# Attention and feed-forward on one core: half of batch 0's first layer in block form, other column pieces of the first weights, squares on either engine, and a new order of all operations

## The chip, the cores and the metric

The kernel runs on one core of a Trainium2 chip. The metric is the device time of one execution in microseconds (us); the median of three runs is compared. The engines are called by the names of the profile: PE (TensorE, matrix products), ACT (ScalarE), DVE (VectorE), POOL (GpSimd, which here issues the loads and waits at a few gates) and SP (SyncE, which issues stores and the transposes by DMA).

## The reference

For 8 batches of 12 heads with 448 positions of 64 numbers, attention with a squared relu in place of the softmax, then a feed-forward network with a gelu:

```python
def _attn_ref(q, k, v):
    S = q.shape[2]
    scale = 1.0 / np.sqrt(q.shape[-1])
    scores = scale * np.matmul(q, k.transpose(0, 1, 3, 2))
    attn = np.maximum(scores, 0.0) ** 2 / S
    return np.matmul(attn, v)

def reference(q, k, v, moe_w_in, moe_w_out):
    a = _attn_ref(q, k, v)                       # (8, 12, 448, 64)
    x = a.transpose(0, 2, 1, 3).reshape(8 * 448, 768)
    h = x @ moe_w_in                             # 768 x 2048
    g = 0.5 * h * (1.0 + erf(h / np.sqrt(2)))
    return g @ moe_w_out                         # 2048 x 768
```

Inputs and output are float32. The kernel multiplies in bfloat16 and sums in float32.

## The kernel before, in words

**Attention.** The heads of a batch form three groups of four, and the 448 keys seven blocks of 64. Q and K are first turned so that the 64 numbers of a head lie on partitions: for batches 0 and 1 by PE (`tp`, lines 619 and 647), with an eviction by ACT or DVE to `qT` and `kT`; from batch 2 on by DMA. A step (`add_steps`) is one group and one block of keys: PE makes the scores in PSUM (`ps`, line 751) with 64-row, 64-column tiles of its array, four products side by side; a relu with the scale takes them to a bfloat16 tile `a_sq` (128 partitions by 896), on ACT (line 768) or DVE (line 770); a square in place follows on DVE (line 777). Batch 0 works in halves of 224 positions. When the seven steps of a group are squared, `add_av` makes the attention product (`pav`, line 824, 28 matmuls), and two copies take it to `xT`, the input of the first layer.

**The first layer** takes 768 numbers to 2048, in 16 column blocks of 128 (called m). It is made in one of two ways.

* Plain (`add_f1`): for one block and all positions, or for two blocks and one half of the positions, six matmuls per block sum over the 768 rows in PSUM (`psh`, line 884), and a gelu on ACT (line 894) writes `h_sb`.
* Block form (`add_early` for batches 1 to 6, `add_blocks` for batch 7): weights and input are each cut in two by two quarters, and seven products of quarters take the place of eight. For this DVE makes sums of weight quarters (`ws`, line 955, by `add_wsums`; one kind is written over a quarter of `win_sb` itself), and sums of input quarters (`t1_x` to `t4_x`, line 998). A unit (`add_unit`) covers two blocks of the upper half of the columns, say 0 and 1, and the two that lie eight further. Its products (`pe`, line 1039, matmuls of 224 columns) share three PSUM banks, and between products ACT or DVE passes a partial sum to `part` (copies, lines 518 and 520; adds on DVE, line 1077); ACT makes four gelus (line 1089). Units come in pairs y = 0, 1; two pairs (h = 0 and h = 1) make a batch. The sums of weights hold one h at a time for the second and fourth kind, so they are made again as h changes.

In the kernel before, batch 0 is plain throughout: blocks 0 to 5 in halves of the positions, blocks 6 to 15 whole.

**The second layer** takes 256 positions at a time (`add_group`, products `pso` at line 1366), in a block form as well.

**Loads.** The first weights come in five pieces of columns (`WINS`, `add_win`), each with three DMAs on POOL's queue; the sums of weights wait for all five.

**The order.** Every operation is created with what it depends on and the engines that may do it. The table `ORDER` then lists all of them: a letter for the engine (P or Q for PE, A for ACT, D for DVE, G for POOL, S for SP; Z is a filler for PE) and the operation's number. Each engine works strictly in this order, and an instruction that waits holds up all behind it. So ACT or DVE is chosen for each relu, copy and eviction by the table alone.

Of the kernel before, what the change touches and what calls it, by code (L numbers as in the profile page):

```python
# [10 lines left out]
AF = mybir.ActivationFunctionType  # L11
# [11 lines left out]
DM = H * D  # L23
# [11 lines left out]
EARLY = (1, 2, 3, 4, 5, 6)  # L35
NB = 512
WINS = (2, 2, 4, 4, 4)
# [15 lines left out]
HALF_M = 6  # L53
# [30 lines left out]
A10 D13 G0 G1594 Z1024 P14 P11 D15 G1 G3 G4 G7 D12 A16 P17 P36 D18 A37 P21 G118 G2 P19 P42 P39 P33  # L84
D22 G117 P23 D20 A43 D40 P48 A34 A49 D24 P25 P54 A55 D26 Z672 P63 P66 D38 A67 D41 D50 P51 A52 P29
D35 P27 D28 D30 D44 P57 D53 D68 P31 D32 A64 A58 P131 P81 G121 A82 P45 A46 A47 P69 A70 D132 D59 G6
P129 P84 A85 P90 A91 G125 G126 D65 G5 D130 P156 D71 D157 P78 A79 Q72 D73 P93 A94 P102 D83 G8 G122
G120 G124 G119 G128 P111 D112 P137 D113 P108 A74 D95 G123 G9 G127 D138 G236 P174 D56 A103 A109 P139
D86 P75 A175 A76 D110 D140 P133 P60 P105 D77 P96 A61 A62 P168 A106 G235 D80 P135 D136 D104 A97 P171
G238 A172 P87 D134 P141 G147 G148 G150 D92 A169 A88 A89 A142 P159 A160 D98 P162 P99 D107 D163 G151  # L90
Q114 A100 A101 P198 A199 D115 D116 P183 A184 P165 A166 D176 P145 A146 S228 S229 G153 P240 A241 D173
D158 G154 D200 P213 A214 P180 D170 A181 P222 P252 A253 D167 S230 P250 A251 D223 P195 D161 A196 P207
D164 D208 P177 P186 A187 D182 D209 D178 D179 P210 D197 P262 A263 D215 A211 G234 P256 P192 D193 P189
P216 P254 A190 A257 S231 P219 A255 D191 D349 D350 D212 P204 A220 P244 S232 S233 D194 A217 P248 A245
A249 D218 D185 P260 A205 P242 A243 D188 P201 A202 D224 G237 G149 G152 A261 G155 D221 D206 P225 D387
D226 D203 A227 D345 D346 D348 P246 A247 D351 P264 G239 G266 P353 P370 A354 P360 P143 A144 G267 P377
P356 D425 D426 A371 D427 A361 A378 D347 P258 A259 D352 P373 D388 P382 P355 A374 P379 D383 D380 P372
P365 A357 P362 D358 P385 A386 D375 A359 D366 D363 P391 P408 A364 G268 P368 A369 P398 P415 P393 P410
D431 A265 D428 A399 D389 P403 D390 A409 A392 P394 D413 P411 A416 P420 D396 D432 A384 A367 P282 Q273
A412 D395 G269 P400 P417 D421 A274 D404 A405 P437 A283 A422 A438 P276 A277 D433 S453 D418 D401 S454  # L100
D434 P291 D429 D435 A292 P406 P423 A424 D430 A407 A402 P439 G270 P288 A289 P285 A286 D293 P297 D298
D440 P441 A442 P315 A316 P279 D284 A414 D287 D436 P300 D290 P443 D444 D275 A280 D281 P445 P447 D278
P309 A301 D446 D448 S451 A397 G271 P303 A419 A381 P294 A376 D469 D470 S455 A310 D295 A304 S456 S457
S458 D305 P312 D311 P449 D450 S452 A313 D302 D314 A296 P321 D471 A322 D323 P324 A325 P306 A307 D308
D317 P473 A474 P339 G459 P327 A328 P475 P477 P336 D299 G462 D472 A340 D329 D476 A337 D338 A478 P330
P318 A331 G272 P333 D334 A319 A320 D332 P479 P498 A499 P492 G465 D341 P489 A490 P481 A493 P495 A496
D335 D326 P342 A343 P507 P504 A505 D480 D482 P485 D344 D561 D562 D564 D563 A508 P565 G460 G461 D509
P582 A583 P572 P589 D494 P585 D586 P567 P584 D500 A566 P568 D573 P591 D570 A590 D592 P594 D587 P577
D599 A569 P483 D578 G463 P601 A588 P618 D486 D595 A602 P574 P597 A598 G464 D600 D491 G466 G467 D575
P603 A576 P620 D484 D619 S488 P580 A581 S635 D606 D497 Q501 A593 S636 A502 S637 D623 P604 P621 D506  # L110
D503 A622 P608 P625 A624 A605 D651 D652 P513 A514 D515 Q510 P522 P610 S638 A596 P627 D626 D628 G641
G644 A609 P613 D611 D653 P630 A511 A512 A523 A571 D614 Q516 A517 P519 D520 P616 P633 D631 A632 D654
D524 A617 P655 A634 P657 P528 D656 D529 P531 A532 D533 S487 G468 P549 A550 D658 P659 D521 A607 D518
P543 A544 P540 A660 D541 P537 A538 P661 P663 D662 A579 D539 P694 P555 D530 D551 A629 P525 A612 A526
D664 A695 D545 D527 P665 D666 A556 D542 P667 A615 D671 P709 A710 D672 P534 P546 S669 P706 A547 D535
A536 A707 P675 D668 P677 P552 S639 S640 G647 P703 D696 P691 D673 G642 D676 D674 D678 P679 A680 D553
A692 P681 D548 D557 P697 D554 P558 G643 G645 G646 D708 A704 P715 D698 P700 D682 D559 P683 A701 D560
P767 P784 D684 D763 A716 D785 A768 D705 D764 P687 P769 P786 P774 D711 D766 P787 A788 D765 A775 D772
P685 A773 G648 D693 D688 D789 G649 S690 P770 A771 D699 P791 D686 P779 A790 Q727 D728 P724 S837 S838
A792 D702 A725 P793 P776 D794 A795 P796 P803 P820 D777 S839 P799 S840 A778 G843 P782 D801 D797 A800  # L120
A783 D804 S670 Q712 P718 G846 D821 D780 A798 A719 A713 A714 P805 P822 P806 D802 P823 D825 A824 Q748
P721 D808 P810 D729 P827 A807 P812 D726 A749 A828 D722 P757 Q730 P829 A811 D717 D853 D854 D830 S689
D813 A731 S841 P832 D833 P857 D858 A826 P818 D732 P815 A809 P835 D720 D816 D855 A831 A819 P859 D860
A758 D759 P861 A817 D862 A836 A834 P896 A897 P733 P739 D740 P863 D856 A734 P742 P905 A906 P745 P865
D898 D864 D866 G650 P867 D735 D750 A781 P869 D868 D723 D870 S872 A814 D873 D874 S842 A746 D747 P920
A921 P736 A737 D738 P751 D876 A743 D744 A752 D753 P877 P879 P911 P754 A878 D880 D875 D741 P908 A755
D756 P881 A882 D909 A912 D922 P883 P893 D894 D884 P899 A900 D910 D895 P760 P926 A761 A762 P923 A924
P885 D886 G849 P887 P902 D913 D901 G844 D888 D965 A927 D967 A903 P917 D907 P889 D890 P969 P986 G845
G847 G848 A918 S1039 D904 Q935 D936 P929 A970 A930 P914 A915 A916 Q941 P971 P988 D966 D968 D919 P976
P993 D925 A987 D991 G850 A994 D937 P972 P989 A990 D977 G851 P981 S892 S1040 D974 A942 P998 A973  # L130
D1003 P1005 P1022 D999 A1000 A1023 P978 D982 D979 A1006 P1007 P1024 D1027 P1008 A992 S1041 A980 Q932
D1010 P995 A1028 P1025 A1026 A933 D996 A997 D1009 P1012 P1029 A1030 D1004 D934 P1014 P1031 D1032
A975 D1013 P1001 A1002 D1015 P1059 D1060 P984 A1016 A985 D931 A1033 S871 G1045 P1020 P1037 A1038
P1034 D1057 P1017 A1021 P950 P1098 P1063 D1055 D1056 D1018 S891 A983 D1035 D951 S1042 S1043 G1048
A1019 P1061 P959 A1099 D1100 P956 D928 D1062 A957 D960 A1036 P938 A939 A940 P1101 D1102 P944 A945
D1058 D946 P1065 A1064 P947 P953 P1119 A1011 D1066 D961 P1067 D958 G852 A948 D1068 A1120 P1069 D943
P1095 A954 D955 D1070 A1096 D1097 D949 D1075 D952 P1122 P1125 A1126 S1073 A1123 P1071 D1072 D1076
P1079 D1080 P1128 D1078 S1074 P1107 A1108 P962 D963 A964 P1110 P1081 D1082 P1083 A1129 A1084 P1104
D1077 D1111 S1044 G1051 G1046 P1113 A1114 P1085 P1173 D1112 A1105 D1106 D1169 P1087 D1109 P1190
P1171 P1188 A1172 A1189 D1086 D1088 P1091 D1103 D1167 D1168 P1178 D1170 D1176 D1092 P1195 A1196  # L140
P1089 P1174 P1191 D1193 A1194 D1130 D1090 Q1134 A1177 A1135 D1115 P1116 D1124 D1179 D1127 A1192
Q1143 D1117 P1183 D1118 A1144 P1200 P1137 A1138 D1175 Q1131 D1201 D1184 A1185 G1047 G1049 P1197
P1180 A1132 A1202 G1050 D1205 D1181 A1182 D1198 D1206 S1241 P1207 P1224 D1208 P1209 P1226 A1225
Q1155 A1156 A1199 P1186 D1212 P1210 D1229 D1145 P1203 A1230 A1204 D1133 P1227 D1228 A1211 P1214
P1231 A1187 P1216 P1233 Q1146 D1139 A1213 D1121 A1232 A1147 D1136 P1140 A1141 Q1149 A1142 D1215
P1219 P1236 D1217 A1218 D1234 A1235 D1150 D1237 A1238 P1222 P1239 G1052 D1220 S1242 Q1152 A1223
D1153 A1240 G1053 A1221 P1270 A1271 P1279 A1280 S1093 S1094 P1276 P1251 A1252 P1158 P1161 D1247
S1243 D1248 A1277 P1253 D1249 D1162 D1157 A1159 P1255 D1254 D1160 P1257 S1244 D1148 D1256 P1259
P1267 P1273 A1274 D1163 D1154 D1151 D1258 D1260 A1268 D1250 P1164 A1165 D1278 P1285 D1281 A1166
D1339 D1340 P1263 A1286 S1245 P1345 P1343 P1360 A1361 P1350 D1272 P1367 P1362 D1287 D1342 D1344  # L150
A1351 P1346 A1368 P1363 A1364 P1372 A1347 D1365 P1261 A1366 D1341 D1275 D1348 P1352 P1369 D1370
D1353 P1355 D1356 S1246 G1595 P1379 P1396 G1054 P1358 D1373 A1371 A1357 D1262 P1375 A1374 A1380
# [252 lines left out]
def kernel(  # L405
# [185 lines left out]
    def add_win(i):  # L591
# [3 lines left out]
        for x in range(m, m + WINS[i]):  # L595
            ld_win[x] = o
# [1108 lines left out]
```

## Time and profile before

| | |
|---|---|
| median of 3 runs | 365.86 us (365.82 to 366.21) |
| the profiled execution | 365.36 us |
| its span, first to last instruction | 363.5 us |
| mean granted TensorE clock | 0.999 |
| instructions | 9137 |
| PE / DVE / ACT busy | 352.7 / 312.9 / 233.4 us |

The profile is one execution. "Busy" counts the time in which at least one instruction of an engine is under way; matmuls overlap in the pipeline, so the mean duration of one is longer than busy time by count. The chain of waits follows the work that ended last backwards. A group is named by the line of the program, the engine and the tiles, output first.

### The profile page before, as it was taken

Reading aid. Unit: us, or ns where it says so; the run is one execution under the profiler, and the core shown is the slowest. Engines: PE = TensorE matmul, PEld = TensorE weight load, DVE = VectorE, ACT = ScalarE, POOL = GpSimd, SP = SyncE. Lnnn points to the kernel's source line nnn. Section 1 sums busy time; section 2 is a strip of 40 time slices with the busy share of each in tenths; the row PEclk is TensorE's granted clock in tenths of the full one; section 3 lists DMA queues with packets and bytes.
Section 4 is the critical chain, followed back from the end, with each engine's and each line's share of the span. In section 5 each row is a group of like instructions: output and inputs, shape, how many; then the busy total and the mean of one; then the engine's idle time right before and its main releaser. Section 6 shows DMA issues by size and latency. Waiting matters only on the chain.

```text
span 363.5 us, 9137 instructions
## 1 busy us (share of the span) xinstructions
PE 352.7 (97%) x3805; PEld 244.2 (67%) x3805; DVE 312.9 (86%) x544; ACT 233.4 (64%) x396; POOL 102.9 (28%) x138
## 2 busy tenths in 40 slices
PE   8889999999999999999999999999999999999995
PEld 4557569855588655886557975678669855798663
DVE  3999988999789899899999799899896999687753
ACT  4998844899846795567675869457854885344200
POOL 8565715284192105610074100470100000000000
PEclk9999999999999999999999999999999999999999
DMA  9999999999999808997199941699900201021213
GB/s 176 200 200 204 202 204 155 172 143 168 155 161 173 157 21 107 142 208 107 56 81 167 183 74 45 94 129 181 136 2 0 88 2 44 3 88 43 88 43 132
DMA packets 124361, 43.01 MB, mean 118 GB/s; under 512 B 102688, under 2 KB 120992, under 8 KB 124320
## 3 DMA queue, kind: packets, MB, share of 16 engines
q0 software_dynamic: 85328, 22.47, 66.4%
q1 hardware_dynamic: 38448, 19.50, 26.3%
q8 instruction: 30, 0.49, 0.6%
q10 hardware_dynamic: 544, 0.46, 0.4%
q14 instruction: 11, 0.09, 0.1%
HBM read 45.61 MB, written 11.01 MB: 156 GB/s over the span
## 4 chain that ended last, share of the span: by engine, by line
PE 83%; DVE 8%; ACT 4%; DMA 2%; issue 1%; POOL 1%; DVEq 0%; POOLq 0%; ACTq 0%
PE pso L1366 36%; PE pe L1039 21%; PE ps L751 8%; PE pav L824 8%; PE psh L884 5%; PE pb L1190 4%; DVE a_sq L777 2%; DMA nq<-in_q_dram 2%; DVE part L1077 2%; DVE part L518 2%; ACT part L520 2%; ACT h_sb L1089 1%; ACT a_sq L768 1%; DVE qT L518 1%; DVE ws L955 0%
## 5 line engine op out<-in xcount | busy, mean ns | idle before, releaser
L768 ACT ACTIVATE a_sq<-ps 128x896 bf16<-128x896 f32 (+1 forms) x151 | 121.9, 861 | 26.1 <-PE ps L751 25.3
L777 DVE TENSOR_TENSOR a_sq<-a_sq 128x896 bf16<-128x896 bf16 x169 | 98.2, 615 | 1.9 <-ACT a_sq L768 1.5
L1366 PEld LDWEIGHTS <-s_sb 128*128 128x128 bf16 x456 | 42.5, 98 | 31.9 <-issue 6.0
L1039 PEld LDWEIGHTS <-win_sb 128*128 128x128 bf16 x576 | 54.4, 98 | 7.9 <-issue 6.3
L751 PE MATMUL ps<-qT,kT 64*64 64x448 bf16 (+1 forms) x756 | 50.0, 338 | 2.4 <-DVE kT L518 0.8
L1077 DVE TENSOR_TENSOR part<-pe,part 128x448 f32<-128x448 f32 x72 | 42.4, 618 | 7.6 <-PE pe L1039 5.9
L1366 PEld LDWEIGHTS <-h_sb 128*128 128x128 bf16 x336 | 31.8, 98 | 22.6 <-issue 4.1
L520 ACT COPY part<-pe 128x448 f32<-128x448 f32 x54 | 27.5, 535 | 29.7 <-PE pe L1039 20.6
L1089 ACT ACTIVATE h_sb<-part 128x448 bf16<-128x448 f32 x72 | 39.9, 580 | 8.8 <-DVE part L1077 8.7
L1039 PEld LDWEIGHTS <-ws 128*128 128x128 bf16 x432 | 41.2, 98 | 2.9 <-issue 2.0
L1366 PE MATMUL pso<-wout_sb,s_sb 128*128 128x384 bf16 (+2 forms) x232 | 41.1, 321 | 0.0
L1366 PE MATMUL pso<-wout_sb,h_sb 128*128 128x384 bf16 x224 | 41.1, 327 | 0.0
L1366 PE MATMUL pso<-t_sb,s_sb 128*128 128x384 bf16 x224 | 41.1, 326 | 0.0
L558 POOL DMA_DIRECT2D nk<-in_k_dram x36 | 34.7, 968 | 10.4 <-DMA wout_sb<-in_moe_w_out_dram 7.9
L770 DVE TENSOR_SCALAR a_sq<-ps 128x896 bf16<-128x896 f32 (+1 forms) x35 | 33.5, 967 | 4.7 <-PE ps L751 4.1
L824 PE MATMUL pav<-a_sq,v_sb 64*64 64x448 bf16 (+1 forms) x756 | 36.4, 329 | 0.5 <-ACT a_sq L768 0.4
L751 PEld LDWEIGHTS <-kT 64*64 64x64 bf16 x756 | 19.0, 105 | 23.8 <-issue 17.9
L1039 PE MATMUL pe<-t_x,win_sb 128*128 128x224 bf16 x288 | 32.6, 259 | 1.3 <-DVE part L518 0.6
L1039 PE MATMUL pe<-t_x,ws 128*128 128x224 bf16 x288 | 31.2, 259 | 0.4 <-ACT part L520 0.4
L708 POOL COPY gate<-qT 128x16 bf16<-128x16 bf16 x10 | 3.0, 299 | 101.1 <-DMA qT<-nq 101.1
L1039 PE MATMUL pe<-xT,win_sb 128*128 128x224 bf16 x288 | 31.5, 259 | 0.0
L1400 DVE TENSOR_TENSOR osb<-pso,p_sb 128x384 f32<-128x384 f32 x42 | 23.2, 552 | 8.8 <-PE pso L1366 7.8
(71 smaller groups left out, 411.8 us busy)
## 6 DMA issues: line engine op xcount, KB each, us to landing
out_dram<-osb SPq DMA_DIRECT2D x19, 384.0 KB, 2.6
nq<-in_q_dram POOLq DMA_DIRECT2D x38, 112.0 KB, 5.9
nk<-in_k_dram POOLq DMA_DIRECT2D x36, 112.0 KB, 5.6
v_sb<-in_v_dram POOLq DMA_DIRECT2D x5, 672.0 KB, 7.5
v_sb<-in_v_dram POOLq DMA_DIRECT2D x9, 224.0 KB, 7.9
win_sb<-in_moe_w_in_dram POOLq DMA_DIRECT2D x8, 192.0 KB, 8.7
wout_sb<-in_moe_w_out_dram POOLq DMA_DIRECT2D x4, 384.0 KB, 12.6
wout_sb<-in_moe_w_out_dram POOLq DMA_DIRECT2D x1, 1536.0 KB, 15.6
```

What stands on the lines that cost most here:

```text
L520: A.copy(dst, src)
L558: nc.gpsimd.dma_start(nk[b][:, g0, :, e], rows[:, e].rearrange("p (i d) -> p i d", d=D))
L751: nc.tensor.matmul(side(ps, e)[64 * j : 64 * j + 64, x * w : x * w + w], kT[r, g, i * 128 + 64 * j : i * 128 + 64 * j + 64], moving, start ...
L768: A.activation(to, x, AF.Relu, scale=c_att)
L770: V.tensor_scalar(to, x, c_att, 0.0, op0=mybir.AluOpType.mult, op1=mybir.AluOpType.max,)
L777: V.tensor_mul(box["a2"][:, :, :used], ar, ar)
L824: nc.tensor.matmul(side(pav[0], e)[o2 : o2 + 64, :w], vt[b][r, 2 * g + e, bass.ts(i, D)], box["a2"][r, e, o : o + w], start=(i == 0), stop ...
L1039: nc.tensor.matmul(bank[name][:, y, z * HS : z * HS + HS], w[:, k, bass.ts(mm, 128)], right()[:, k], start=first and k == 0 and z == 0, st ...
L1077: V.tensor_add(get(to), ps(name), get(other))
L1089: A.activation(h_ring()[:, m : m + 2, o + half[c].start : o + half[c].stop], src().rearrange("p (x n) -> p x n", x=2), AF.Gelu,)
L1366: nc.tensor.matmul(box[bank][:, n0:n1], left()[:, kf], right()[:, kf, n0:n1], start=bool(need) and kf == 0, stop=kf == K2 - 1, skip_group_ ...
L1400: V.tensor_add(out()[:, n0:n1], box[bank][:, n0:n1], other()[:, n0:n1])
```

## The change

Four things change together.

1. Batch 0 joins the batches of the block form with the half h = 1: blocks 4 to 7 and 12 to 15, two units. The other eight blocks stay plain: 0, 1 and 8 to 11 in halves of the positions, 2 and 3 whole. The sum of weights that overwrites a quarter of `win_sb` waits for these plain products where it must. The sums for h = 1 are made for batch 0 and used by batch 1 first; in the kernel before they were made for batch 1.
2. The pieces of the first weights hold other columns: blocks 0 and 1, 6 and 7, 8 to 11, 2 to 5, 12 to 15. Their sizes stay.
3. The square may be done by ACT, as an activation, or by DVE.
4. The table of the order is new from its first line to its last, with 1618 operations for 1596.

```diff
-EARLY = (1, 2, 3, 4, 5, 6)
+EARLY = (0, 1, 2, 3, 4, 5, 6)
-WINS = (2, 2, 4, 4, 4)
+WINS = ((0, 2), (6, 8), (8, 12), (2, 6), (12, 16))
-HALF_M = 6
+HALF_M = (0, 8, 10)
 ORDER = """
-A10 D13 G0 G1594 Z1024 P14 P11 D15 G1 G3 G4 G7 D12 A16 P17 P36 D18 A37 P21 G118 G2 P19 P42 P39 P33
...
+G0 G1616 G1 G3 G4 G7 D13 Z1024 A10 G118 A16 G2 P14 D15 P11 D12 P17 D18 P19 D20 P42 A43 P36 A37 P33
...
     def add_win(i):
-        m = sum(WINS[:i])
-        c = slice(128 * m, 128 * (m + WINS[i]))
-        o = dma(lambda: load_win(c), DM * 128 * WINS[i] * 4, issues=3)
-        for x in range(m, m + WINS[i]):
+        m0, m1 = WINS[i]
+        c = slice(128 * m0, 128 * m1)
+        o = dma(lambda: load_win(c), DM * 128 * (m1 - m0) * 4, issues=3)
+        for x in range(m0, m1):
             ld_win[x] = o
...
             def fn_mul(e_, box=box, used=used):
                 ar = box["a2"][:, :, :used]
-                V.tensor_mul(box["a2"][:, :, :used], ar, ar)
+                if e_ == "ACT":
+                    A.activation(ar, ar, AF.Square)
+                else:
+                    V.tensor_mul(ar, ar, ar)
...
-            o3 = sch.add((("DVE", d, d + 0.12),), fn_mul, [o2], bias=bias)
+            d2 = 0.07 + 2 * used / 1200
+            o3 = sch.add(
+                (("DVE", d, d + 0.12), ("ACT", d2, d2 + 0.12)), fn_mul, [o2], bias=bias
+            )
...
+    PLAIN = [(m + x, h) for m in HALF_M for x in range(2) for h in range(2)]
+    PLAIN += [(m, None) for m in (2, 3)]
...
     def add_early(b):
-        done = [o for (bb, *_), o in F1.items() if bb < EARLY[0]]
+        done = [F1[0, m, h] for m, h in PLAIN] if b else []
...
-        for h in ((0, 1), (1, 0))[at % 2]:
+        for h in ((1,), (1, 0), (0, 1))[0 if b == 0 else 2 - at % 2]:
...
-    for m in range(0, HALF_M, 2):
+    for m in HALF_M:
         add_f1(0, m, 0, bias=F1_BIAS)
...
-    for m in range(0, HALF_M, 2):
+    for m in HALF_M:
         add_f1(0, m, 1, bias=F1B_BIAS)
-    for m in range(HALF_M, KF):
+    for m in (2, 3):
         add_f1(0, m, bias=F1B_BIAS)
+    flow = [o for o in add_early(0)]
```

Line numbers of the changed kernel are higher than those of the profile by 1 (from line 518 on), 4 (the square on DVE stands at 781, on ACT at 779), 7 (from 824), 9 (from 998) and 10 at the end.

Counted over the whole program: 61 of the 169 squares now stand on ACT; 57 relus stand on DVE where 35 did (halves and split ones counted as they are issued) and 125 on ACT where 151 did. PE has 48 `psh` matmuls of 448 columns fewer and 84 `pe` matmuls of 224 more. POOL's list of loads is the same in kind and size, row by row.

Two places show how the order differs. The first is DVE around the last squares of batch 1's attention (`a_sq`), where the sums of first weights (`ws`, `win_sb`) and of inputs (`t_x`) come in. Before:

```order
L770 TENSOR_SCALAR a_sq<-ps 128x896
L777 TENSOR_TENSOR a_sq<-a_sq 128x896
L955 TENSOR_TENSOR ws<-win_sb 128x3x512
L955 TENSOR_TENSOR ws<-ws,win_sb 128x1536
L777 TENSOR_TENSOR a_sq<-a_sq 128x896 x8
L955 TENSOR_TENSOR ws<-win_sb 128x3x512
L518 CAST xT<-pav 128x448 x2
L998 TENSOR_TENSOR t_x<-xT 128x672
L998 TENSOR_TENSOR t_x<-xT,t_x 128x672 x2
L955 TENSOR_TENSOR ws<-win_sb,ws 128x1536
```

In the changed kernel, at the same place:

```order
L771 TENSOR_SCALAR a_sq<-ps 128x896
L781 TENSOR_TENSOR a_sq<-a_sq 128x896 x3
L962 TENSOR_TENSOR ws<-win_sb 128x3x512
L781 TENSOR_TENSOR a_sq<-a_sq 128x896 x3
L962 TENSOR_TENSOR ws<-ws,win_sb 128x1536
L1007 TENSOR_TENSOR t_x<-xT 128x672
L519 COPY part<-pe 128x448
L962 TENSOR_TENSOR ws<-win_sb 128x3x512
L1086 TENSOR_TENSOR part<-pe,part 128x448
L781 TENSOR_TENSOR a_sq<-a_sq 128x896
L962 TENSOR_TENSOR win_sb<-win_sb 128x3x512
L962 TENSOR_TENSOR ws<-win_sb,ws 128x1536
```

The last squares of batch 1 now stand between the sums for batch 0's block products, and a copy and an add of those products stand ahead of the very last one.

The second place is ACT at the end of batch 1's attention, with its relus (`a_sq` from `ps`), gelus (`h_sb`), casts of the attention product (`xT`) and copies of block products (`part`). Before:

```order
L768 ACTIVATE a_sq<-ps 128x896 x2
L894 ACTIVATE h_sb<-psh 128x2x224
L894 ACTIVATE h_sb<-psh 128x448
L768 ACTIVATE a_sq<-ps 128x896
L894 ACTIVATE h_sb<-psh 128x2x224
L520 CAST xT<-pav 128x448
L894 ACTIVATE h_sb<-psh 128x448
L520 CAST xT<-pav 128x448
L894 ACTIVATE h_sb<-psh 128x448
L520 COPY part<-pe 128x448
```

In the changed kernel:

```order
L769 ACTIVATE a_sq<-ps 128x896
L521 COPY part<-pe 128x448
L769 ACTIVATE a_sq<-ps 128x896
L521 CAST xT<-pav 128x448 x2
L769 ACTIVATE a_sq<-ps 128x896
L779 ACTIVATE a_sq<-a_sq 128x896 x2
L521 COPY part<-pe 128x448 x4
L521 CAST xT<-pav 128x448 x2
L1098 ACTIVATE h_sb<-part 128x2x224 x3
```

The last relus are followed by two squares on ACT, for which the last attention product of batch 1 waits, and copies of block products of batch 0 stand before and behind them.

More of the change, by code (lines that the diff above doesn't have):

```diff
@@ L89 @@
[L89 to L113, printed above, removed]
@@ new lines @@
+D1110 P1111 D1100 P1113 G1074 D1128 A1211 D1215 P1165 A1194 G1075 D1198 D1112 S1115 A1199 A1166
+A1167 D1114 P1138 D1190 D1192 S1264 S1265 Q1153 S1096 P1200 P1217 P1196 P1213 A1139 A1154 D1140
+A1218 Q1177 A1201 D1227 A1197 P1159 A1160 P1205 A1214 P1222 D1191 A1216 P1229 P1246 P1219 D1223
+A1224 S1116 D1206 D1178 A1247 D1220 P1231 S1266 P1248 D1251 S1267 A1230 G1617 P1232 P1249 A1161
+A1221 P1202 A1233 D1234 A1235 P1225 A1250 D1228 A1207 D1158 D1203 A1226 P1236 P1253 A1152 P1238
+D1146 D1237 D1239 P1208 P1241 P1244 A1209 A1204 D1155 P1255 A1240 D1242 A1243 A1252 P1171 S1268
@@ new lines @@
+D1254 D1256 Q1168 A1169 P1258 D1172 P1261 A1257 Q1174 A1245 A1262 D1259 A1260 P1162 P1295 A1173
+A1163 G1076 P1183 A1184 D1175 P1273 D1269 A1274 D1270 P1275 A1164 P1301 D1271 A1179 D1176 P1180
+A1302 A1303 D1276 P1277 P1279 D1296 D1185 D1278 P1281 P1289 A1181 A1182 D1272 D1170 D1280 D1282
+A1290 P1307 D1308 P1186 A1187 D1188 D1361 P1292 A1293 D1294 P1298 P1285 A1297 P1365 P1382 D1286
+D1362 D1364 A1299 D1300 P1367 A1383 P1372 P1389 A1366 D1370 A1291 D1373 A1390 D1363 P1283 A1371
+D1284 P1384 D1387 P1385 P1368 A1369 P1304 Q1313 A1305 D1399 D1386 P1377 P1394 D1306 D1395 A1396
@@ new lines @@
+A1388 P1401 P1418 A1419 P1391 D1378 P1403 P1420 A1402 P1374 D1309 P1404 P1421 D1400 D1406 D1423
+A1424 P1408 P1425 D1375 D1392 A1376 D1475 A1405 A1422 A1393 D1409 P1397 A1398 D1426 A1379 P1410
+D1314 P1427 D1428 P1380 A1381 S1288 P1430 A1429 D1411 A1412 P1413 D1414 P1340 D1431 A1341 Q1310
+A1311 D1435 D1315 P1355 A1356 P1328 A1329 P1416 P1433 A1417 P1439 P1352 S1287 P1343 D1312 A1434
+D1436 D1438 A1432 P1322 D1437 D1353 A1415 P1441 D1323 A1440 P1443 P1325 D1344 P1316 D1442 A1444
+P1346 A1347 P1445 P1331 D1326 A1407 D1327 D1324 P1337 D1446 A1342 D1457 A1332 A1333 P1447 A1348
@@ new lines @@
+P1555 A1554 P1557 A1494 D1518 P1521 A1514 D1556 P1543 D1541 A1542 P1546 A1491 D1522 D1524 A1525
+D1547 A1548 S1474 A1558 P1559 P1526 P1529 D1530 S1453 D1560 A1531 P1536 A1537 D1544 A1545 P1561
+D1562 D1527 A1528 P1563 D1564 P1519 A1520 D1569 P1565 S1567 D1570 P1573 A1574 D1566 S1568 D1571
+P1575 D1572 P1577 D1576 D1578 P1579 P1581 D1580 P1583 D1582 P1585 D1591 D1584 S1587 D1589 D1590
+D1586 S1588 P1593 P1595 A1594 D1596 P1597 A1598 S1609 P1599 D1592 P1601 D1600 P1603 D1602 P1606
+S1610 D1604 S1611 P1605 D1607 S1612 D1608 S1613
@@ L1595 @@
     add_v(3, 0, G)
-    flow, plans = [], {}
+    plans = {}
     F1B = {2: 1, 3: 2, 4: 3, 5: 4, 6: 5, 7: 6}
```

124 lines of the change are left out of this document (63 added, 61 removed).

## The prediction, made before the changed kernel was run

> **What bounds the kernel now.** I read the page's first part, then a table by stages, then the chain of waits, the groups of instructions and the waits. The first part gives the span and the engines' shares.
>
> ```profile
> span 363.5 us, 9137 instructions
> PE 352.7 (97%) x3805; PEld 244.2 (67%) x3805; DVE 312.9 (86%) x544; ACT 233.4 (64%) x396; POOL 102.9 (28%) x138
> ```
>
> By its average TensorE (PE) is the bound. The table by stages says where that is not the whole story; its columns are the stretch, its length, and each engine's busy time with its instructions.
>
> ```profile
> 4.90:26.00 21.10, 17.48 (x461) 12.08 (x463) 19.16 (x38) 19.28 (x29) 14.59 (x21) 1.00 1.39 196
> 26.00:49.10 23.10, 23.02 (x310) 14.63 (x305) 21.67 (x37) 18.62 (x30) 13.48 (x17) 1.00 1.29 204
> 49.10:80.00 30.90, 30.21 (x304) 23.31 (x297) 27.91 (x42) 21.14 (x40) 15.07 (x20) 1.00 1.68 166
> 80.00:130.00 50.00, 49.45 (x513) 33.12 (x512) 44.98 (x80) 37.83 (x63) 19.44 (x25) 1.00 1.51 153
> 130.00:330.00 200.00, 198.74 (x2024) 140.31 (x2022) 179.66 (x315) 128.57 (x223) 36.55 (x47) 1.00 0.72 91
> ```
>
> From 4.9 to 26 us PE lacks 3.6 us, while VectorE (DVE) and ScalarE (ACT) are each 91% busy: this stretch is theirs. From 26 us on PE is busy almost throughout, but DVE stays at 90 to 94% up to 130 us. Only after that has it room. The chain of waits names the milestones (start, length, what).
>
> ```profile
> 47.85 2.77 PE pav L824 x56
> ...
> 55.88 1.15 PE pe L1039 x12
> 57.02 1.14 PE psh L884 x6
> ...
> 74.96 1.30 PE pso L1366 x8
> 76.26 0.69 PE ps L751 x12
> 76.96 1.41 PE pso L1366 x8
> ...
> 340.20 19.65 PE pso L1366 x128
> ```
>
> The 56 matmuls at 47.85 are the last two attention products of batch 1; the last one starts half of 2.77 us later, at 49.2. The run ends in 19.65 us of unbroken second-layer products, where nothing else matters.
>
> **The change, part by part.** *The block form on PE.* Removed are 48 matmuls of 448 columns, added are 84 of 224. Six of the wide ones take 1.14 us (0.190 each), twelve of the narrow ones 1.15 (0.0958 each). That is 84 x 0.0958 - 48 x 0.190 = 8.05 - 9.12 = -1.07 us, all on PE, which sets the end.
>
> *Changes of kind on PE.* A run of eight products of 1.30 us takes 1.41 next to a score product: 0.11 us for a change between the 64-row attention products and the 128-row ones. Counted in the order, PE changes kind 138 times before and 132 times after: -6 x 0.11 = -0.66 us. As the price comes from one pair, its bounds are 0 and -1.3.
>
> *The work of DVE and ACT.* These rows price it (busy, mean of one); a price is busy time by count.
>
> ```profile
> L777 DVE TENSOR_TENSOR a_sq<-a_sq 128x896 bf16<-128x896 bf16 x167 | 97.6, 618 | 1.8 <-ACT a_sq L768 1.5
> L768 ACT ACTIVATE a_sq<-ps 128x896 bf16<-128x896 f32 x124 | 108.7, 930 | 23.9 <-PE ps L751 23.3 <-PE pav L824 0.4
> L768 ACT ACTIVATE a_sq<-ps 128x448 bf16<-128x448 f32 x27 | 13.3, 547 | 2.2 <-PE ps L751 2.0
> L770 DVE TENSOR_SCALAR a_sq<-ps 128x896 bf16<-128x896 f32 x26 | 28.3, 1087 | 3.2 <-PE ps L751 2.7
> L1077 DVE TENSOR_TENSOR part<-pe,part 128x448 f32<-128x448 f32 x72 | 42.4, 618 | 7.6 <-PE pe L1039 5.9 <-ACT h_sb L1089 1.2
> L518 DVE COPY kT<-tp 128x896 bf16<-128x896 bf16 x5 | 3.1, 619 | 0.0
> L518 DVE CAST xT<-pav 128x448 bf16<-128x448 f32 x14 | 8.3, 619 | 4.2 <-ACT xT L520 3.2 <-PE pav L824 0.8
> L518 DVE CAST xT<-pav 128x224 bf16<-128x224 f32 x3 | 1.1, 386 | 0.2 <-PE pav L824 0.2
> L520 ACT CAST xT<-pav 128x448 bf16<-128x448 f32 x28 | 13.9, 538 | 9.5 <-PE pav L824 7.1 <-DVE xT L518 2.4
> L955 DVE TENSOR_TENSOR ws<-win_sb 128x1536 bf16<-128x1536 bf16 x2 | 1.9, 952 | 0.0
> L998 DVE TENSOR_TENSOR t_x<-xT 128x672 bf16<-128x672 bf16 x12 | 5.9, 500 | 0.0
> L894 ACT ACTIVATE h_sb<-psh 128x448 bf16<-128x448 f32 x16 | 8.7, 555 | 3.8 <-PE psh L884 3.7
> ```
>
> Over the run 61 of 169 squares leave DVE at 0.584 us (-35.6) and 19 wide relus come to it at 1.09 (+20.7). Four input sums (+2.0), six adds (+3.5), seven copies (+4.3) and small shifts make DVE about 5 to 10 us lighter. ACT gains 61 squares. No ACT square is in the trace; the bounds are 0.58 (DVE's square) and 0.93 (mean ACT relu of that width), and I take the relu's 0.877 by count, since engine and width are the same: +53.5, less 15 relus (-13.2) and 11 half ones (-5.4), plus evictions (about +6): 41 us more, 64% to 75% of the span. For the end this matters only where an engine has no room.
>
> That is up to the last attention product of batch 1, which stands after the same PE work in both kernels, counted in columns. Counted in the order up to the last square it needs, DVE has 5 fewer evictions of K and Q (-3.1), 4 more narrow and 2 fewer wide casts (+0.3), 3 more wide and 1 more half relu (+3.9), 5 fewer squares (-2.9), a weight sum (+1.0), 4 input sums (+2.0), and a copy and an add (+1.2): +2.3 us. ACT has the 5 evictions (as its relu, +4.4), 4 wide casts for 4 narrow ones (+0.7), 5 squares for 5 wide relus (0), 3 half relus (+1.5), a copy (+0.5), 2 fewer gelus (-1.1): +6.0.
>
> The room: in the 44.2 us from 4.9 to 49.1 DVE is busy 19.16 + 21.67 = 40.8, ACT 19.28 + 18.62 = 37.9. DVE has 3.4 us free, ACT 6.3; the change asks for 2.3 and 6.0. Some of that free time is waiting on others, which an order can shorten but not remove:
>
> ```profile
> DVE a_sq L770 <- PE ps L751: 1.0, 2, 0.6
> ...
> ACT a_sq L768 <- PE ps L751: 2.6, 5, 1.1
> ACT h_sb L894 <- PE psh L884: 2.6, 5, 0.9
> ```
>
> With no idle at all the milestone would be on time or 0.3 us early. At the old shares of work (DVE 92%, ACT 86%) DVE is late by 2.5 and ACT by 7, though ACT lacked work there rather than time; at 91%, its share in the crowded stretch, ACT is late by 43.9 / 0.91 - 44.2 = 4.0. I take +0.8, with about half of the old waits left (free time 1.7 on DVE, 1 on ACT): nearer the low end, because the relus that DVE now makes itself give it work that waits on no ACT. Bounds -0.3 and +4.0.
>
> *The weights.* Queue order and sizes are the same; the pieces hold other columns. The sum of weights needs all of them: last issue 32.0 us, at most 10.5 to land, 42.5. Before, the first sum starts at 42.8.
>
> ```profile
> L493 POOL DMA_DIRECT2D win_sb<-in_moe_w_in_dram x5: 626/630/632, 15.3 to 32.0; - x5
> ...
> DMA to landing us min/median/max: 7.5/8.5/10.5
> L955 DVE TENSOR_TENSOR ws<-win_sb x2: 950/952/953, 42.8 to 48.9; 128x1536 bf16<-128x1536 bf16 x2
> ```
>
> After, by the same prices 1.9 us more DVE work stands ahead of that sum, so it costs nothing; behind it three squares of batch 1 are queued, for which PE waits. If it were a microsecond late, so would PE be.
>
> *After 49.2 us* the longest waits of PE that the profile names are short ones, while DVE and ACT pass on block products:
>
> ```profile
> PE pe L1039 <- ACT part L520: 0.6, 3, 0.2
> PE pe L1039 <- DVE part L518: 0.6, 2, 0.4
> ```
>
> DVE is lighter after 130 us, tighter up to 100; ACT is tighter throughout. I put 0, with -1.2 (those waits gone) and +1.2 (as much again) as bounds.
>
> *Sum:* -1.07 - 0.66 + 0.8 + 0 = -0.93 us. The profiled execution took 365.36 us, 1.9 around its span; it goes to 364.4. The median of the runs shown is 365.86, half a microsecond above; it goes to 364.9.
>
> **The rivals.** *A: the start is the bound, and it ends slower.* Between 4.9 and 49.2 us both elementwise engines are asked for 43 to 44 us of 44.2. If they keep at most 92 to 93%, the last attention product of batch 1 starts at 52.2 instead of 49.2, and 3.0 - 1.7 = +1.3 us remain: 367.2. It decides from 51.6 on (1.7 won, 0.7 to be told from no change). For it speak DVE's 90 to 94% up to 130 us, so that a delay is not made up soon; against it, that PE's waits on ACT and DVE lie in the first 26 us, where a new order can place work better.
> The Trainium skill has a rule for this rival (ScalarE: Activation LUTs, Rules for kernel authors): do relu and multiplication on VectorE, not on ScalarE. It speaks against moving squares to ACT, and the rows agree, 0.584 us against 0.877; by that page's 186 ns + 0.833 ns per element less 93 ns of overlap one would be an estimated 0.84 us, 2 us less over 61 squares.
>
> *B: no change.* The start eats the 1.7 us: late by 1.0 to 2.4, 365.2 to 366.6, about 365.9. The same comes out if the block form's passes make PE wait twice for 0.6 us, as it does in the rows above.
>
> *C: the new order does better than the pieces.* The milestone is 0.3 us early and the later waits go: -1.7 - 0.3 - 1.2 = -3.2, 362.7. For it speaks the 3.6 us that PE lacks in 4.9 to 26; against it, that both engines must then be without idle.
>
> The row for the last rival:
>
> ```profile
> L1496 ACT ACT_TABLE_LOAD x1 | 1.3, 1283 | 1.8 <-issue 1.8
> ```
>
> *D: the change does not do what it says,* the squares on ACT asking for a table load each. One load takes 1.28 us; 61 of them would be over 78 us. The order has one load, as before, so I give it under 1%.
>
> **How the numbers follow.** A measurement of this kernel tells about 0.2%, 0.7 us, from no change. Forecast 364.9 with its own range 363.3 to 365.1: 40%; C: 10%; B: 27%; A: 23%. Faster by over 0.2% means below 365.13: 50% with C; within 27%, slower 23%. The range takes A with the 0.2 us by which its price may be low, and takes in C with as much below it: 362.4 to 367.4.
>
> **What would show it.** Right: the last attention product of batch 1 starts at 49.5 to 50.5 us; 132 changes of kind; 12 psh matmuls of 448 columns; DVE near 305 us, ACT near 274; ACT squares of 0.8 to 0.9 us by count. Wrong: that product after 51.6 (A); ACT squares over 1 us; a DVE wait on the weights at the first sum; stalls past 50 us that grow by more than 1.2.

## The result, and the profile after

The changed kernel takes 360.36 us (359.83 to 360.48), the kernel before in the same comparison 365.84: a ratio of 0.9845, interval 0.9828 to 0.9862. That is 5.5 us less where 0.9 were forecast, and below the range. The profiled execution took 360.24 us. In a_refit_dve and a_refit below, one execution each had a lower granted clock (0.753 and 0.853) and is left out, and as the latter was the profiled one, no trace of a_refit is read.

The page's first part of the changed kernel:

```profile
span 358.5 us, 9223 instructions
PE 350.0 (98%) x3841; PEld 248.0 (69%) x3841; DVE 305.6 (85%) x515; ACT 270.3 (75%) x437; POOL 102.9 (29%) x138
```

The work on DVE and ACT came out near the forecast (305 and 274 us). The table by stages, columns as in the prediction:

```profile
4.90:26.00 21.10, 17.97 (x445) 11.95 (x444) 19.12 (x37) 18.83 (x29) 14.58 (x21) 1.00 1.38 194
26.00:49.10 23.10, 22.37 (x335) 16.62 (x336) 22.39 (x40) 22.35 (x36) 13.47 (x17) 1.00 1.29 203
49.10:80.00 30.90, 30.90 (x323) 25.53 (x321) 30.44 (x48) 26.76 (x52) 13.88 (x18) 1.00 1.59 158
80.00:130.00 50.00, 50.00 (x530) 33.75 (x528) 45.93 (x78) 43.55 (x68) 20.07 (x27) 1.00 1.61 164
130.00:330.00 200.00, 200.00 (x2039) 142.98 (x2037) 171.85 (x286) 151.75 (x245) 37.10 (x47) 1.00 0.68 90
```

Two things stand out. From 49 us on PE lacks nothing: before, it lacked 0.69, 0.55 and 1.26 us in these three stretches. And up to 130 us DVE is fuller than before, not emptier: busy for 30.44 of 30.90 us from 49 to 80 us, where it was busy for 27.91. Only from 130 us on does it have less to do, 171.85 us where it had 179.66. The chain of waits of the changed kernel around the milestone:

```profile
47.04 3.56 PE pe L1048 x36
50.59 1.45 PE pav L831 x28
52.04 7.96 PE pe L1048 x82
```

The last attention product of batch 1 starts at 50.59 instead of 49.2, so the start cost 1.4 us, and all of the gain lies behind it. The 1.4 is the difference of two single executions, and the start varies: the run a_cpl below has the same work in the same order up to this product and starts it at 49.98. From the product to the end the kernel before takes 314.3 us and the changed one 307.9. This part is steady: a_wins and a_dve5 below, whose order behind the product is the same, take 307.9 too. The start times of PE's matmuls in the trace tell where. A gap is the time from one start to the next beyond what the columns take (0.0958 us for 224, 0.190 for 448). After 49 us, in us:

| gaps of PE | before | after |
|---|---|---|
| between two block products (`pe`) | 3.26, ten of 0.29 to 0.41 | 0.06 |
| between two score steps (`ps`) | 0.95, three | 0.02 |
| at changes of kind between scores and layers | 9.92, one of them 0.58 at 70.6 | 8.77, none over 0.2 |
| all others | 0.61 | 0.62 |
| sum | 14.74 | 9.47 |

The view of waits names hardly any of it, since most of these gaps are hidden in the modelled ends of the matmuls. For PE after 49 us it has three rows before (1.6 us, two of them in the prediction) and none after. What the gaps are is told by the waits of DVE and ACT. The groups that copy block products to `part`, in the kernel before (after the bar: busy, mean of one, then idle time ahead of them and what ended it):

```profile
L520 ACT COPY part<-pe 128x448 f32<-128x448 f32 x54 | 27.5, 535 | 29.7 <-PE pe L1039 20.6 <-DVE part L518 6.2 <-DVE part L1077 2.9
L518 DVE COPY part<-pe 128x448 f32<-128x448 f32 x18 | 11.1, 620 | 3.4 <-ACT part L520 2.6 <-PE pe L1039 0.9
```

And in the changed kernel:

```profile
L521 ACT COPY part<-pe 128x448 f32<-128x448 f32 x53 | 26.4, 541 | 8.9 <-PE pe L1048 6.2 <-DVE part L519 2.5
L519 DVE COPY part<-pe 128x448 f32<-128x448 f32 x25 | 15.0, 618 | 1.5 <-PE pe L1048 0.9 <-ACT part L521 0.6
```

A copy takes its data from PE's bank, so why does ACT's copy wait for one of DVE's? 6.2 + 2.9 + 2.6 = 11.7 us of such waits stand before, 2.5 + 0.6 = 3.1 after. One of them in time order, in the kernel before (start, length, what, and in brackets the idle time ahead and who ended it):

```profile
198.32 1.60 PE L1039 MATMUL pe<-t_x,ws 128*128 128x224 bf16 x15
198.34 0.61 DVE L777 TENSOR_TENSOR a_sq<-a_sq 128x896 bf16<-128x896 bf16 x1
...
198.81 0.53 ACT L520 COPY part<-pe 128x448 f32<-128x448 f32 x1 [1.18 <-PE pe L1039]
199.37 0.62 DVE L518 COPY part<-pe 128x448 f32<-128x448 f32 x1 [0.42 <-ACT part L520]
...
200.05 0.26 PE L1039 MATMUL pe<-xT,ws 128*128 128x224 bf16 x1
200.06 0.10 PEld L1039 LDWEIGHTS <-ws 128*128 128x128 bf16 x1 [0.29 <-issue]
```

Both copies read the same PSUM tile, `bank["c"]`: ACT the half of unit y = 1, DVE the half of y = 0. DVE's product was done at 198.2 us and DVE was free at 198.95. Still its copy starts at 199.37, 0.03 us after ACT's has ended. The product that waits for it starts at 200.05, and PE has idled 0.29 us. In the table of the order ACT's copy (A994) is listed ahead of DVE's (D977).

This repeats. In the kernel before, 16 reads of block products start 0.03 or 0.09 us after an earlier listed read of the same tile's other half by the other engine; had they gone as soon as their product and their engine allowed, they would have started some 13 us earlier in all. In the changed kernel there are 7, with some 3 us. There is no exception: of 85 reads in the kernel before that are listed behind a read of the tile's other half by the other engine, and of 81 such reads in the changed kernel, none starts sooner than 0.03 us after the end of the read listed first. Of the ten gaps and the one of 0.58, nine end with such a read, and the one at 288.9 us is a step behind one; the one at 250.9 has two weight sums ahead of its copy in DVE's queue.

### The profile page after: what moved, and what is told of

The parts are those of the page before. It is cut to its first block, busy times and chain, and to the rows that moved or that the text cites. A ratio compares the mean times of both kernels' runs of the same rounds, so it can differ in the third digit from the quotient of the medians.

```text
span 358.5 us, 9223 instructions
## 1 busy us (share of the span) xinstructions
PE 350.0 (98%) x3841; PEld 248.0 (69%) x3841; DVE 305.6 (85%) x515; ACT 270.3 (75%) x437; POOL 102.9 (29%) x138
## 4 chain that ended last, share of the span: by engine, by line
PE 92%; ACT 5%; DVE 2%; issue 0%; DVEq 0%; ACTq 0%
PE pso L1375 37%; PE pe L1048 30%; PE ps L752 9%; PE pav L831 8%; PE pb L1199 4%; ACT a_sq L769 3%; PE psh L891 2%; PE spin L1510 1%; DVE a_sq L781 1%; DVE a_sq L771 1%; ACT xT L521 0%; PE tp L620 0%; PE fill L1677 0%; ACT a_sq L779 0%; ACT qT L521 0%
## 5 line engine op out<-in xcount | busy, mean ns | idle before, releaser
L769 ACT ACTIVATE a_sq<-ps 128x896 bf16<-128x896 f32 (+1 forms) x125 | 106.7, 893 | 14.5 <-PE ps L752 14.2
L781 DVE TENSOR_TENSOR a_sq<-a_sq 128x896 bf16<-128x896 bf16 (+1 forms) x108 | 63.8, 615 | 2.1 <-ACT a_sq L769 1.9
L1048 PEld LDWEIGHTS <-win_sb 128*128 128x128 bf16 x624 | 59.5, 98 | 2.7 <-issue 1.5
L771 DVE TENSOR_SCALAR a_sq<-ps 128x896 bf16<-128x896 f32 (+1 forms) x57 | 55.5, 988 | 2.6 <-PE ps L752 2.2
L779 ACT ACTIVATE a_sq<-a_sq 128x896 bf16<-128x896 bf16 x61 | 57.2, 959 | 0.5
L1098 ACT ACTIVATE h_sb<-part 128x448 bf16<-128x448 f32 x78 | 43.2, 580 | 9.9 <-DVE part L1086 9.7
L1086 DVE TENSOR_TENSOR part<-pe,part 128x448 f32<-128x448 f32 x78 | 45.5, 620 | 5.3 <-PE pe L1048 3.6
L1048 PEld LDWEIGHTS <-ws 128*128 128x128 bf16 x468 | 44.1, 98 | 3.5 <-issue 2.9
L1048 PE MATMUL pe<-xT,win_sb 128*128 128x224 bf16 x312 | 34.1, 259 | 0.0
L1048 PE MATMUL pe<-t_x,ws 128*128 128x224 bf16 x312 | 33.2, 259 | 0.0
```

The costliest lines, as they stand in the source:

```text
L769: A.activation(to, x, AF.Relu, scale=c_att)
L771: V.tensor_scalar(to, x, c_att, 0.0, op0=mybir.AluOpType.mult, op1=mybir.AluOpType.max,)
L779: A.activation(ar, ar, AF.Square)
L781: V.tensor_mul(ar, ar, ar)
L1048: nc.tensor.matmul(bank[name][:, y, z * HS : z * HS + HS], w[:, k, bass.ts(mm, 128)], right()[:, k], start=first and k == 0 and z == 0, st ...
L1086: V.tensor_add(get(to), ps(name), get(other))
```

## The experiments

Runs named a_ start from the changed kernel, runs named b_ from the kernel before. Times with the kernel before stand at 365.6 to 365.8 us in each comparison; ratios are to it. Two theories ran against each other. *Relief*: the gaps went because squares left DVE. *Order*: they went because the list is another one; after the first four runs this became the *rule of tiles*: an access to a PSUM tile waits for every access to that tile listed ahead of it on another engine, also where the halves differ.

| run | us | ratio (interval) |
|---|---|---|
| changed kernel | 360.36 | 0.9845 (0.9828 to 0.9862) |
| a_dve61 | 384.84 | 1.0524 (1.0501 to 1.0548) |
| b_act56 | 388.34 | 1.0612 (1.0590 to 1.0633) |
| a_plain0 | 362.75 | 0.9915 (0.9900 to 0.9930) |
| a_wins | 360.47 | 0.9856 (0.9841 to 0.9871) |
| b_list | 365.58 | 0.9992 (0.9984 to 1.0001) |
| a_cpl | 363.62 | 0.9943 (0.9930 to 0.9957) |
| a_dvepol | 392.73 | 1.0739 (1.0725 to 1.0754) |
| b_pol | 400.43 | 1.0956 (1.0941 to 1.0971) |
| b_refit_same | 363.90 | 0.9945 (0.9931 to 0.9958) |
| b_refit | 363.28 | 0.9932 (0.9919 to 0.9945) |
| a_refit_dve | 364.60 | 0.9977 (0.9967 to 0.9988) |
| a_dve5 | 362.67 | 0.9916 (0.9903 to 0.9929) |
| a_late56 | 363.17 | 0.9928 (0.9914 to 0.9943) |
| a_refit | 362.34 | 0.9903 (0.9887 to 0.9920) |

### The squares alone, in both directions

All 61 squares of ACT back on DVE at their places (a_dve61; a word of the order per square), and in the kernel before 56 of its 126 squares of batches 2 to 7, evenly spread, given to ACT at theirs (b_act56):

```diff
-A53
+D53
```

```diff
-            o3 = sch.add((("DVE", d, d + 0.12),), fn_mul, [o2], bias=bias)
+            o3 = sch.add(
+                (("DVE", d, d + 0.12), ("ACT", d2, d2 + 0.12)), fn_mul, [o2], bias=bias
+            )
```

Expected of a_dve61:

> The changed kernel with all 61 squares of ACT given back to DVE at the same places of the order; nothing else differs. Theory 1 (the squares on ACT relieve DVE, so that block products no longer wait for a pass): DVE is asked for 61 x 0.58 = 36 us more, 341 us in all, the waits come back and the time is 365 us or more. Theory 2 (the new order alone removed the waits; where the squares run is incidental): within 1 us of 360.4.

Expected of b_act56:

> The kernel before with 56 of its 126 squares of batches 2 to 7, evenly spread, given to ACT at the same places of its order; no block form for batch 0, no new order. Theory 1: DVE is 33 us lighter, most of the ten waits of block products after 49 us go, 361.5 to 363.5 us. Theory 2: within 0.7 us of 365.8, or slower, since ACT's gelus and copies then stand behind squares that the order did not foresee.

Both are much slower, by 24.5 us against the changed kernel and by 22.8 against the kernel before. By itself a_dve61 speaks for relief: it is over the 365 us that relief gave, and gaps between block products are back (4.9 us after 49 us). But most of its loss stands elsewhere. The waits of PE, first of a_dve61, then of b_act56 (us in all, times, longest):

```profile
PE pav L831 <- DVE a_sq L781: 4.2, 5, 1.9
PE ps L752 <- DVE a_sq L771: 4.1, 9, 1.1
```

```profile
PE ps L751 <- ACT a_sq L768: 5.6, 9, 1.7
PE pav L830 <- ACT a_sq L778: 3.7, 3, 2.1
```

A list fits one placing of the squares; with another, whichever engine got them is late. In b_act56 DVE had 27 us less work, and fourteen gaps between block products stood there all the same (5.1 us). Relief had given 361.5 to 363.5 us for it. So relief in its plain form, less work on DVE and the waits go, falls.

### The other two parts of the change

The changed kernel with batch 0 plain throughout, its list kept as far as it goes (a_plain0), and with the old column pieces (a_wins):

```diff
-    flow = [o for o in add_early(0)]
+    flow, rest0 = [], []
+    for m in (12, 13, 14, 15, 4, 5, 6, 7):
+        rest0.append(add_f1(0, m, bias=F1B_BIAS))
+    add_wsums(LAST_UNITS, rest0[:4], (1,), True)
```

```diff
-WINS = ((0, 2), (6, 8), (8, 12), (2, 6), (12, 16))
+WINS = ((0, 2), (2, 4), (4, 8), (8, 12), (12, 16))
```

> The changed kernel with the first layer of batch 0 plain throughout (blocks 4 to 7 and 12 to 15 whole, in the places of the block products), the rest of the order kept. Theory 1 or 2: the block form is worth its shorter products alone, 1.1 us, so 361.4 us. Theory 3 (the passes and sums of the block form are what makes the start late by 1.4 us): the last attention product of batch 1 comes back to about 49.5 us and the time is 360 us or less.

> The changed kernel with the pieces of the first weights in the old columns (0 and 1, 2 and 3, 4 to 7, 8 to 11, 12 to 15), order kept. If the new columns matter, the products of blocks 8 to 11 wait for a piece that is issued one place later, some 3 us, and PE is up to 3 us late: 361 to 363 us. If they don't, 360.4 within 0.4.

a_plain0 is 2.4 us slower than the changed kernel. One wait is of my own making: a gelu placed too late at 50.3 us, in the view of waits

```profile
PE psh L890 <- ACT h_sb L900: 1.4, 1, 1.4
```

and a gap of 1.59 us in the starts. It lies ahead of the last attention product of batch 1, which starts at 51.55 and not at the 49.5 of theory 3. Less this gap it would be 49.96, about where a_cpl below has it with the block form (49.98), so nothing speaks for the passes of the block form as what makes the start late. From that product to the end a_plain0 takes 309.0 us against 307.9, close to the 1.07 that the block form was priced at. The gaps between block products stayed away, so they do not hang on the block form of batch 0. The column pieces make no difference.

### Only the list, every queue as it was

b_list takes the kernel before and lists eleven words elsewhere so that the queue of each engine stays word for word the same; seven pairs are turned round. a_cpl does the opposite to the changed kernel, in four places (A539, the word that follows A627 on ACT, goes along behind it). One place of each:

```diff
-G850 A994 D937 P972 P989 A990 D977
+G850 D937 P972 P989 D977 A994 A990
```

```diff
-D1018 A1031 P1034 P1051 D1048
+D1018 P1034 P1051 D1048 A1031
```

> The kernel before, with eleven words of its order listed at another place so that the work queued on each engine stays word for word as it was; only which of two engines' instructions is listed first changes, for seven pairs that read the two halves of one PSUM tile. Theory of pairs: of the two reads, the one listed later waits for the one listed earlier when they are on two engines, though they touch different halves; ten of the kernel before's stalls after 49 us are products that wait for such a pass, and here the six at 61.7, 64.3, 105.0, 112.3, 119.0 and 200.1 us go (0.29 + 0.30 + 0.36 + 0.30 + 0.30 + 0.29 = 1.84 us): about 364.0 us, 0.4% to 0.6% faster than the kernel before, the other four stalls still there. Theory of relief (the ten waits went because squares left VectorE, which is as full here as before): no change, within 0.2% of the kernel before, and the stalls stay or move by a few us.

> The changed kernel, with five words of its order listed at another place, again with the queue of every engine unchanged: five reads of one half of a PSUM tile are listed behind the read of the other half on the other engine instead of ahead of it. Theory of pairs: four new stalls of TensorE of 0.3 to 0.7 us each, at products that wait for a pass, 2.1 us in all: about 362.4 us, 0.4% to 0.7% slower than the changed kernel. Theory of relief: VectorE has as little to do as in the changed kernel, so the time stays at 360.4 us within 0.2%.

a_cpl is 3.3 us slower than the changed kernel (2.1 expected), though no engine does anything else or in another order. Around A1031:

```profile
205.54 1.15 DVE L519 COPY part<-pe 128x448 f32<-128x448 f32 x2
...
206.27 0.53 ACT L521 COPY part<-pe 128x448 f32<-128x448 f32 x1 [1.50 <-DVE part L519]
...
206.85 0.35 PE L1048 MATMUL pe<-t_x,win_sb 128*128 128x224 bf16 x2 [0.44 <-ACT part L521]
206.85 0.19 PEld L1048 LDWEIGHTS <-win_sb 128*128 128x128 bf16 x2 [0.60 <-issue]
```

ACT sits idle 1.50 us until DVE has read the tile's other half, and PE waits for ACT. New gaps stand at 206.9, 252.3 and 253.3 us (0.50 to 0.60), and at 116.9 us one of 1.23, where a score relu was queued behind a held copy. Relief expected no change, so it falls a second time. It is shown that the listing alone, with every engine's queue as it was, makes such gaps.

b_list, though, changed nothing, against my expectation. Its trace says why: the wait turned round with the pair. A357, now first, waits for P379 instead, a product into the other half that is listed ahead of it: that ends at 60.70, A357 starts at 60.73, and D380 then starts 0.03 us after A357's end. So the rule covers products too, and turning a pair is not removing it. That made the rule of tiles what it is above.

### Refitted lists

a_dvepol and b_pol move DVE's and ACT's words among each other with no square on ACT, so that no product should wait long, but by a rule that knew only pairs of reads:

> The changed kernel with all 61 squares of ScalarE back on VectorE, as in the run that took 384.8 us, but here the words of VectorE and ScalarE are moved among each other (42 copies and passes change between these two engines) so that no product waits long for them; TensorE's order is kept. VectorE has some 330 us of work again, ScalarE some 225. Theory of pairs (the squares on ScalarE are worth little by themselves; what counts is that no pass that a product needs is held): 361 to 363 us. Theory of relief: the waits come back, since VectorE is as full as in the kernel before: 364 us or more.

> The kernel before with the words of VectorE and ScalarE moved among each other in the same way (37 copies and passes change between the two engines), no square on ScalarE and TensorE's order kept. Theory of pairs: the ten stalls of 3.3 us go, and little else changes: 362 to 363 us, 0.7% to 1.0% faster than the kernel before, which leaves 1.5 to 2.5 us to the changed kernel for its block form (1.07), its six fewer changes of kind (0.66) and what it does at the start. Theory of relief: VectorE is as full as in the kernel before, so at best a third of the ten stalls goes: 364.5 us or more.

Both are far off (gaps after 49 us of 40.9 and 48.9 us): their lists ran into products of other halves, and in b_pol a sum of second-layer weights (D425) moved ahead of the load it needs held DVE for 9.0 us, up to 52.7. They tell nothing of the theories. The next three use the whole rule and keep the sums behind their loads. Of b_refit's edit the words at the pair of the timeline above, where the copy of y = 0 goes to ACT:

```diff
-G850 A994 D937 P972 P989 A990 D977 G851 P981
+G850 P972 A994 A977 P989 G851 P981
```

> The kernel before, all work on the engine where it was (no square on ScalarE) and TensorE's order kept; only the places of VectorE's and ScalarE's instructions in the listing and in their own queues are moved. Theory of tiles (an access to either half of a PSUM tile waits for every access to that tile that is listed ahead of it on another engine, products into the other half too; the earlier try at seven pairs turned the wait round instead of taking it away): a listing can be had in which seven or more of the ten stalls go, 2.3 to 2.9 us, so 362.7 to 363.4 us. Theory of relief: the waits come from VectorE's load, which is the same here: 365.0 to 366.0 us, or more.

> As the run before, but 31 copies, evictions and one attention cast may also change between VectorE and ScalarE (16 leave ScalarE, 15 leave VectorE), no square among them. Theory of tiles: all ten stalls go, 3.3 us, and a little of the other waits: 361.7 to 362.7 us, so that 1.3 to 2.3 us are left for what the changed kernel does on TensorE (1.73 by the sum). Theory of relief: 364.5 us or more.

> The changed kernel with all 61 squares of ScalarE back on VectorE and the places of both engines' instructions refitted under the rule of tiles (35 copies, evictions and casts change engine; TensorE's order kept). Theory of tiles: the squares on ScalarE are worth only what the start needs; 361.8 to 363.2 us, against 384.8 with the squares simply put back. Theory of relief: VectorE is as full as in the kernel before, the ten waits come back: 364 us or more.

b_refit_same, with all work on its engine and no square moved, is 1.7 us faster than the kernel before by the medians, 2.0 by the ratio; the gaps between block products fall from 3.26 to 1.08 us. b_refit, where 31 copies, evictions and casts may change engine, gains 2.3 to 2.5; these gaps are 0.57 us, none over 0.2. The pair of the timeline, now both on ACT (L519 in this kernel):

```profile
198.35 1.31 PE L1038 MATMUL pe<-xT,ws 128*128 128x224 bf16 x12
198.48 0.97 ACT L519 COPY part<-pe 128x448 f32<-128x448 f32 x2 [0.18 <-PE pe L1038]
...
199.50 0.35 PE L1038 MATMUL pe<-xT,win_sb 128*128 128x224 bf16 x2
```

The two copies run back to back and PE goes on without a gap. In these two runs DVE is as full as before (311.5 and 312.1 us against 312.9). Both fell short of my numbers by 0.5 to 0.6 us. In a_refit_dve the gaps between block products are 0.18 us with no square on ACT and DVE at 326.2 us (90%), so these gaps need no relief; yet it is 4.2 us slower than the changed kernel: by its time it lies on the side of relief. 1.0 us of that is the start (the milestone at 51.63), 1.4 one wait of an attention product at 99.9 us for a cast on DVE, 0.7 gaps between score steps.

### What the squares on ACT are worth

a_dve5 puts back only the five squares ahead of the milestone; a_late56 keeps these five and puts back the other 56, refitted; a_refit is its control, refitted with 60 squares on ACT. A word of a_dve5's edit, one of five:

```diff
-A206
+D206
```

> The changed kernel with only the five squares of ScalarE that stand ahead of the last attention product of batch 1 put back on VectorE at their places, nothing else moved. VectorE gets 5 x 0.58 = 2.9 us more before 50 us, where it has little room, ScalarE 4.4 us less. If these five squares on ScalarE are what keeps the start from being later still: that product starts 1.5 to 2.9 us later and the time is 361.9 to 363.3 us. If the start waits for ScalarE instead: the time is 360.4 us or less.

> The changed kernel with the five squares of ScalarE ahead of batch 1's last attention product kept there and the other 56 back on VectorE, and the places of both engines' instructions refitted as in the run with all 61 back (364.6 us, where 1.0 us of the 4.2 was lost by 49 us and 1.4 us in one wait at 99.9 us). If the 56 late squares are worth nothing once the listing is fitted: 360.4 to 361.4 us, as the changed kernel or nearly. If VectorE's load after 49 us does cost: 362.0 to 364.0 us, the stalls spread over score products and the attention products, not at block products.

> The control for it: the changed kernel with 60 squares on ScalarE (34 of the words of squares stand on other squares or places), refitted in the same way. If the refit by itself helps or hurts nothing: 360.0 to 361.0 us. If it hurts by itself (it moves work past waits that the rule of tiles does not tell of), the time is over 361.5 us and the other refitted runs are too high by about as much.

a_dve5 is 2.3 us slower than the changed kernel. The chain of waits in it:

```profile
45.25 1.69 DVE a_sq L781 x3
...
49.80 0.63 DVE part L519
50.43 0.04 issue
50.47 2.46 PE pe L1048 x24
52.93 1.45 PE pav L831 x28
```

DVE's squares push back a copy of a block product, and the milestone goes from 50.59 to 52.93: 2.3 us, which is the whole loss. That is the price with the rest of the list as it stands. In refitted lists the five are worth less: a_refit_dve, without them, has the milestone at 51.63 and a_late56, with them, at 50.90, and the medians are 1.4 us apart (1.8 by the ratios). a_refit lies 2.0 us above the changed kernel, which is put down to the refit, though 34 of its squares also stand at other places. a_late56 lies 0.8 us above this control, the two intervals touching: the 56 late squares are worth 0 to 1.7 us together. If the refit costs as much in the kernel before, which was not tried, what b_refit and b_refit_same gain is a lower bound for the list's share.

## Why the prediction was wrong, step by step

- *The block form on PE, -1.07:* right. There are 12 `psh` matmuls of 448 columns as forecast, and a_plain0 takes 1.1 us more from the milestone on.
- *Changes of kind, -0.66:* right. The gaps at changes fell by 1.15 us, of which 0.48 (0.58 less 0.10) is a held copy at 70.6 us; 0.67 is left.
- *The work of DVE and ACT:* right over the run. The ACT square is dearer than taken, also by count:

```profile
L781 DVE TENSOR_TENSOR a_sq<-a_sq 128x896 bf16<-128x896 bf16 x106 | 63.0, 620 | 1.9 <-ACT a_sq L769 1.7
L779 ACT ACTIVATE a_sq<-a_sq 128x896 bf16<-128x896 bf16 x61 | 57.2, 959 | 0.5
```

  57.2 / 61 = 0.94 us against 0.877 taken and against 0.59 on DVE. (From start to start, one straight behind another, it is 0.840, by the start times in the trace.) The Trainium skill's rule to keep relu and multiplication off ScalarE (ScalarE: Activation LUTs, Rules for kernel authors) agrees with the single price. As advice it fails here: five such squares on ACT, each 0.35 us dearer, save 2.3 us in this list, as DVE has no room there.
- *The start, +0.8:* +1.4 in the profiled executions, within its bounds, and 50.59 is just past the 49.5 to 50.5 named as a sign of being right. The medians are 5.5 us apart where these two spans are 5.0, so +1.4 is likely above the usual. Rival A was wrong in that the rest did not stay lost.
- *After 49.2 us, 0 with bounds of 1.2:* **this step failed.** It was -3.2 (block products) - 0.48 (the copy at 70.6) - 0.93 (score steps) = -4.6 us. I had bounded what could go by PE's named waits on copies, 1.2 us. PE's idle time in the table by stages, 2.5 us from 49.1 to 330 us, would not have been enough either. Both miss a gap that is shorter than the modelled tail of a matmul. The waits that carried it stood in the groups of ACT and DVE, as idle time that ended with the other engine's `part`. I did not ask why a copy from PSUM should wait for a copy on another engine.

The sum as measured: -1.07 - 0.67 + 1.4 - 4.6 = -4.9, against 358.5 - 363.5 = -5.0 in the spans. Rival C had the direction (later waits go) with a quarter of the size, and an early milestone that did not come.

How much of the 4.6 is the list: the 3.7 at block products needs no relief, as a_cpl makes such gaps by the listing alone and two refitted lists, b_refit and a_refit_dve, take nearly all of them away with no square on ACT. How much time the list wins by itself is open; b_refit_same and b_refit, with no square on ACT, won 1.7 to 2.5 us of the 5.5. The 0.93 at score steps may go with the squares: such gaps are 0.02 in the changed kernel and in a_dve5, 0.76 and 1.17 in a_refit_dve and b_refit, which have none on ACT. But a_cpl, with all 61 there, has one of 0.37 at 111.4 us, so the list can bring these too; this is argued from the traces, not tried by itself. Open is why the program orders accesses to different halves. The Trainium skill (PSUM — Partial Sum Buffer, PSUM bank collisions raise a hardware error) says that two engines must not be in one 2 KiB bank, on the same 32 partitions, at once, reads against reads included, and that different banks run clean. The halves here, 512 float32 values each, are two banks, so by that page the wait would not be needed; no run here gave the halves tiles of their own.

## What to carry to other kernels

Before a term is put at nothing because the bounding engine shows few waits, read the idle time of the engines that feed it, and ask of each releaser whether it could have a reason: a copy that waits for a copy on another engine shows an ordering between them. Where a table lists the work as here, two engines reading parts of one PSUM tile follow the list, so put both reads on one engine or list them as they become ready. Moving work to a slower engine pays where the full engine sets a milestone (five squares, 2.3 us in this list, 1.4 to 1.8 in refitted ones), not by the total moved (56 squares, 1.7 us at most by the control).

## What had not been expected of the hardware

The ACT square in place, bfloat16 from SBUF, takes no less than the relu of the same width from PSUM in the changed kernel (0.94 us by count against 98.9 / 109 = 0.91; from start to start, one straight behind another, 0.840 against 0.797):

```profile
L769 ACT ACTIVATE a_sq<-ps 128x896 bf16<-128x896 f32 x109 | 98.9, 939 | 12.2 <-PE ps L752 11.9
```
